# Left-over tokens carried by the last chunk of a batch, and two MoE weights loaded through two hardware queues

## The chip, the cores and the metric

The kernel runs on one core of a Trainium2 chip. The metric is the time of one execution in microseconds of the device; lower is better. The core's 16 DMA engines take work from three kinds of queue that matter here: GpSimd's software queue (q0 in the profile), SyncE's hardware queue (q1) and ScalarE's hardware queue (q10).

## What is computed

The inputs q, k, v are float32 of shape (4, 6208, 256): B = 4 batches, N = 6208 tokens, C = 256 channels. An attention between channels is followed by a mixture-of-depths layer, in which only the 128 tokens of a batch with the highest score pass a small MLP:

```python
qn = q / (norm(q, axis=1) + 1e-06);  kn = k / (norm(k, axis=1) + 1e-06)
a = softmax(kn.transpose(0, 2, 1) @ qn / tau)        # 256 x 256 for each batch
x = v @ a                                            # (4, 6208, 256)
scores = x @ w_gate;  out = x.copy()
for b in range(B):
    top = indices of the 128 highest scores[b]
    ye = maximum(x[b, top] @ w1, 0) @ w2             # 256 -> 1024 -> 256
    out[b, top] = x[b, top] + sigmoid(scores[b, top])[:, None] * ye
```

## The kernel before

**Tiling.** A batch of 6208 tokens is cut into `NFULL` = 6 chunks of `CHUNK` = 1024 tokens and `REM` = 64 left-over tokens. A chunk is laid over 128 partitions with `RPP` = 8 consecutive tokens each, so that a partition reads 8 KB in one piece from memory; the load casts to bfloat16 and writes 4 KB to a partition. The 64 left-over tokens are a seventh piece (chunk index `NFULL`): one token on each of 64 partitions, in small tiles of their own (`rem_pool`), loaded by a DMA of its own (L179). All loads of q, k and v are issued by GpSimd (`emit_load`, L168 to L187). The chunk (q, k) of the last batch that is used last is loaded in two halves of four tokens a partition (L185).

**Two passes.** Pass 1 reads q and k of a batch and sums three products over all tokens (L303, L305, L307): q against k, and the squared norms. From these come the 256 x 256 weights `a` (`softmax_stages`). Pass 2 transposes v on TensorE (L414), copies it to `vt_sb` (L418, L420), multiplies by `a` (L485) and copies the float32 result into a `stage` tile (L493, L491), which SyncE stores (`emit_store`, L559): 8 KB for each of 128 partitions, 1 MB a chunk. The left-over tokens have a stage tile and a store of their own (64 KB). A score for each token comes from L439; `select_stages` narrows down a threshold in seven rounds on VectorE and turns the 128 hits into row numbers (`idx`); GpSimd gathers those rows of v (L660), `mlp_stages` runs the MLP, and GpSimd scatters the updated rows over the stored output (L729), which has to come after the stores of that batch.

**Order of work.** The order on TensorE is the list `plan`, written out by hand. The order of loads follows from it (`units`); `pump` issues loads ahead within limits: four (q, k) chunks, six v chunks, two left-over pieces of each kind, and in all 11 pieces ahead. Side work (softmax, selection, MLP) is slipped in between by `spent`. With the batches numbered 0 to 3, the names in the code are H = 1, E = 2, L = 3. Chunk 3 of batch 1 and all of batch 2 are not stored when they are ready but put in `deferred`, and `flush_deferred` (L779) stores them behind the last loads of v: the first of them in four pieces, of which the first and third wait for loads named by their place from the end of `units` (L784). The stores of batch 3 follow. The last two chunks of batch 1 (`LATE`) come at the very end: there the MLP's update isn't scattered but added to the stage tile by a matmul against a one-hot matrix (`late_onehot`, `late_mm`, `late_pair`), and the last of them is stored in two halves (`next_late`, L882).

**The start.** `emit_weights` loads w1 (1 MB, L218) and w2 (1 MB, L224) through SyncE's queue into two stage tiles, and ScalarE casts them (L220, L225). The gate vector of 1 KB comes through ScalarE's queue (L211).

Of the kernel before, what the change touches and what calls it, by code (L numbers as in the profile page):

```python
# [17 lines left out]
P = 128  # L18
# [8 lines left out]
def kernel(  # L27
# [30 lines left out]
    ST_BUFS = 8  # L58
    VT_BUFS = 22
    EARLY = 4  # L60
# [27 lines left out]

    def view(t, b, ci):
        if ci < NFULL:  # L90
            return t[b, ci * CHUNK:(ci + 1) * CHUNK, :].rearrange("(p s) c -> p s c", s=RPP)
        return t[b, NFULL * CHUNK:N, :]

# [55 lines left out]
    plan += T[6:8] + W + T[8:10] + S[:6] + T[10:] + rest[2:3] + [("side",)] + S[6:]  # L149
    rest = rest[3:]  # L150
    units = []
    for op in plan:
        if op[0] in ("p1", "T"):
            u = ("qk", op[1], op[2]) if op[0] == "p1" else ("v", op[1], op[2][0])
            if u not in units:
                units.append(u)
    loaded = {}
    load_inst = {}
    state = {"next": 0, "qk": 0, "v": 0, "qkr": 0, "vr": 0}
    ahead = [0]  # L160
    limit = {"qk": QK_BUFS, "v": V_BUFS, "qkr": 2, "vr": 2}

    def bucket(kind, ci):
        return kind if ci < NFULL else kind + "r"

    halved = ("qk", B - 1, NFULL - 1)

    def emit_load(u):  # L168
        kind, b, ci = u
        tiles = []  # L170
        for nm, src in ((("q", q), ("k", k)) if kind == "qk" else (("v", v),)):
            if ci < NFULL:
                pool = qk_pool if kind == "qk" else v_pool
                t = pool.tile([P, RPP, C], BF16, name=f"{nm}_ch")
                if u != halved:
                    ins = nc.gpsimd.dma_start(out=t, in_=view(src, b, ci))  # L176
            else:
                t = rem_pool.tile([P, 1, C], BF16, name=f"{nm}_rem")
                ins = nc.gpsimd.dma_start(out=t[:REM, 0, :], in_=view(src, b, ci))  # L179
            tiles.append(t)  # L180
        if u == halved:
            h = RPP // 2
            for half in (slice(0, h), slice(h, RPP)):
                for t, src in zip(tiles, (q, k)):
                    ins = nc.gpsimd.dma_start(out=t[:, half, :], in_=view(src, b, ci)[:, half, :])  # L185
        loaded[u] = tiles
        load_inst[u] = ins  # L187

    def pump(most=1000):
        while state["next"] < len(units) and most > 0:  # L190
            u = units[state["next"]]
            bk = bucket(u[0], u[2])
            if state[bk] >= limit[bk] or ahead[0] >= AHEAD:
                return
            emit_load(u)
            ahead[0] += 2 if u[0] == "qk" else 1
            state[bk] += 1
            state["next"] += 1
            most -= 1

    def consumed(u):
        state[bucket(u[0], u[2])] -= 1
        ahead[0] -= 2 if u[0] == "qk" else 1
        pump()
# [5 lines left out]
    wg_row = moe.tile([P, D], F32, name="gy")[0:1, :]  # L210
    nc.scalar.dma_start(out=wg_row, in_=moe_w_gate.partition_broadcast(1))  # L211

    def emit_weights():


        assert C * F == P * RPP * C
        raw = st_pool.tile([P, RPP, C], F32, name="stage").rearrange("p a c -> p (a c)")
        nc.sync.dma_start(out=raw.rearrange("p (k n) -> p k n", n=F), in_=moe_w1.rearrange("(k p) n -> p k n", p=P))  # L218
        for kc in range(C // P):
            nc.scalar.copy(w1_sb[:, kc, :, :],  # L220
                           raw[:, kc * F:(kc + 1) * F].rearrange("p (n f) -> p f n", f=NFC))
        raw = st_pool.tile([P, RPP, C], F32, name="stage").rearrange("p a c -> p (a c)")
        raw = raw.rearrange("p (f n) -> p f n", n=D)
        nc.sync.dma_start(out=raw, in_=moe_w2.rearrange("(p f) n -> p f n", f=NFC))  # L224
        nc.scalar.copy(w2_sb, raw)  # L225

    emit_weights()


# [29 lines left out]
    nc.vector.memset(wrow, 1.0)  # L259
    nc.vector.memset(wrow[:, :, RPP - 1:NCOL - 1:RPP], float(CHUNK - RPP + 1))  # L260
    nc.vector.memset(wrow[:, :, NCOL - 1:NCOL], 0.0)
# [5 lines left out]
    for i in range(NSTEP):  # L267
# [11 lines left out]
    nc.vector.tensor_copy(rhs[:, NCOL + 2:NCOL + 3], iota_col)  # L279
    ones_col = const.tile([P, NCOL], BF16)  # L280
# [7 lines left out]
    def p1_steps(b, ci):  # L288
# [3 lines left out]
        s_ps, g_ps = acc[b]  # L292
        qt, kt = loaded[("qk", b, ci)]
        rows = RPP if ci < NFULL else 1
        parts = P if ci < NFULL else REM

        def step(s):
            first = ci == 0 and s == 0
            last = ci == NFULL
            qs, ks = qt[:parts, s, :], kt[:parts, s, :]  # L300
# [106 lines left out]
    def p2_transpose(b, g, on_act=False):  # L407
        ci, s0, n = g
        parts = P if ci < NFULL else REM
        vt = loaded[("v", b, ci)][0]  # L410
        vt_ps = vt_psum()
        for j in range(n):
            for cc in range(2):
                nc.tensor.transpose(vt_ps[:, cc, j, :parts], in_=vt[:parts, s0 + j, cc * P:(cc + 1) * P],  # L414
                                    identity=ident_b[:parts, :parts])
# [116 lines left out]
    def late_onehot(idx):  # L532

        base = float(H * N + LATE[0] * CHUNK)
        at = moe.tile([P, 1], F32, name="late_at")
        nc.vector.tensor_copy(at, idx)
        nc.vector.tensor_scalar(out=at, in0=at, scalar1=-base, scalar2=1.0 / RPP, op0=ALU.add, op1=ALU.mult)
        onehot = moe.tile([P, len(LATE), RPP, P], BF16, name="late_onehot")
        for i in range(len(LATE)):
            at_row = moe.tile([P, RPP], F32, name=f"late_at_row{i}")  # L540
            nc.vector.tensor_scalar(out=at_row, in0=iota_row[:, 0:RPP], scalar1=-1.0 / RPP, scalar2=at,
                                    op0=ALU.mult, op1=ALU.add)
            nc.vector.tensor_tensor(out=onehot[:, i, :, :], in0=iota_row[:, None, :].to_broadcast([P, RPP, P]),
                                    in1=at_row[:, :, None].to_broadcast([P, RPP, P]), op=ALU.is_equal)
            if i + 1 < len(LATE):
                nc.vector.tensor_scalar(out=at, in0=at, scalar1=-float(P), scalar2=None, op0=ALU.add)
        late_moe.append(onehot)

    def emit_store(b, ci, rows=(0, RPP), count=1):
        st = stage_of[(b, ci)]  # L550
        pieces = []
        if ci == NFULL:
            pieces.append((view(out, b, ci), st[:REM, 0, :]))
        else:
            n = (rows[1] - rows[0]) // count
            for r in range(rows[0], rows[1], n):
                pieces.append((view(out, b, ci)[:, r:r + n, :], st[:, r:r + n, :]))
        for dst, src in pieces:
            ins = nc.sync.dma_start(out=dst, in_=src)  # L559
# [10 lines left out]
    def select_stages(b):  # L570
# [55 lines left out]
        with nc.allow_low_precision(reason="counts of at most 49 are whole in bf16"):  # L626
# [25 lines left out]
        fl = moe.tile([P, 1], F32, name="fl")  # L652
        nc.vector.scalar_tensor_tensor(out=fl, in0=toff, scalar=float(b * N + NFULL * CHUNK) - 0.5,
                                       in1=mps[:, NCOL + 1:NCOL + 2], op0=ALU.is_lt, op1=ALU.mult)
        idx = moe.tile([P, 1], I32, name="idx", bufs=3)
        nc.vector.tensor_scalar(out=idx, in0=mps[:, NCOL + 2:NCOL + 3], scalar1=fl, scalar2=toff,
                                op0=ALU.max, op1=ALU.add)
        yield
# [120 lines left out]
    def flush_deferred():  # L779
# [3 lines left out]
        emit_store(*deferred.pop(0), count=4)  # L783
        for piece, u in ((first, units[-4]), (first + 2, units[-3])):  # L784
            tc.add_manual_dep(
# [8 lines left out]
    def do_p1(b, ci, s):  # L794
        if s == 0:
            pump()
            using(("qk", b, ci))
        steps = p1_steps(b, ci)
        steps[s]()
        spent(0.43)  # L800
        if s == len(steps) - 1:
            consumed(("qk", b, ci))

    def do_transpose(b, g, on_act=False):
        using(("v", b, g[0]))
        vts[(b, g)] = p2_transpose(b, g, on_act)
        if g[1] == 4 or g[0] == NFULL:
            consumed(("v", b, g[0]))
        spent(0.11 * g[2])
# [131 lines left out]
```

## Time and profile before

| | |
|---|---|
| time, three runs | 261.95 us (261.92 to 263.41) |
| span of the profiled run | 260.1 us |
| busy: TensorE matmul, VectorE, ScalarE, GpSimd | 78%, 49%, 32%, 21% |
| mean granted TensorE clock | 0.947 |
| read from HBM, written to HBM | 78.91 MB, 25.95 MB |
| loads of q, k, v of whole chunks | 72, of which 2 in halves |
| loads of left-over tokens | 12, of 32 KB written to the core's memory each |
| stores of left-over tokens | 4, of 64 KB each |

A page of the profile has the busy share of each engine in 40 equal slices (a digit is tenths), the DMA queues with their packets and bytes, the chain of work that ended last, and the instructions in groups with their line, their operands, the mean time of one and the idle time ahead of them. A load's size is given by what it writes, so a chunk of q counts as 512 KB although 1 MB is read for it.

### The profile page before, as it was taken

The numbers are of one execution on the slowest core, as the hardware profiler recorded it, in microseconds if no ns is written. First come the engines' busy times: TensorE is split into PE (matmuls) and PEld (weight loads), VectorE is DVE, ScalarE is ACT, GpSimd is POOL, SyncE is SP. The second block draws the span as 40 slices with busy tenths as digits, with TensorE's granted clock in tenths as the row PEclk, the third lists the DMA queues.
The fourth block names the chain that finished last, engine by engine and source line by source line (L and its number), as shares of the span: only waits on it lengthen the run. The fifth ranks groups of instructions, "written<-read, shape, count | busy, mean of one in ns | idle before, by whom it ended". The sixth has DMA issues, their size and how long they took to land.

```text
span 260.1 us, 6113 instructions
## 1 busy us (share of the span) xinstructions
PE 201.7 (78%) x2586; PEld 177.3 (68%) x2586; DVE 126.9 (49%) x474; ACT 84.3 (32%) x149; POOL 55.6 (21%) x104
## 2 busy tenths in 40 slices
PE   0199668889938688698997888799999878889920
PEld 0088557789927476598996677698999668568710
DVE  0300003624403366622436888666685865887830
ACT  3700000167720000107770100434110964878010
POOL 7104124121110023222300325230334003001110
PEclk9999999999976589689999999999999999999995
DMA  7999999999999999999999999999999999999980
GB/s 240 262 213 212 212 212 214 215 214 281 317 317 317 304 213 213 214 212 210 292 316 273 214 212 223 212 213 214 212 210 212 217 257 419 402 412 391 415 369 1
DMA packets 17181, 66.84 MB, mean 257 GB/s; under 512 B 2050, under 2 KB 3587, under 8 KB 14211
## 3 DMA queue, kind: packets, MB, share of 16 engines
q0 software_dynamic: 12384, 38.93, 75.0%
q1 hardware_dynamic: 4768, 27.53, 26.2%
q8 instruction: 20, 0.33, 0.4%
q14 instruction: 7, 0.05, 0.0%
q10 hardware_dynamic: 2, 0.00, 0.0%
HBM read 78.91 MB, written 25.95 MB: 403 GB/s over the span
## 4 chain that ended last, share of the span: by engine, by line
DMA 57%; PE 16%; issue 15%; DVE 6%; POOL 2%; POOLq 1%; ACT 0%
DMA k_ch<-in_k_dram 22%; DMA q_ch<-in_q_dram 18%; DMA v_ch<-in_v_dram 12%; PE s_ps L303 4%; PE o_ps L485 4%; DMA out_dram<-upd,idx 3%; DMA out_dram<-stage 2%; PE g_ps L307 2%; PE g_ps L305 2%; PE vt_ps L414 2%; DVE cnt L610 1%; DVE cmp L606 1%; PE sc_ps L439 1%; DVE junk L322 1%; PE m_ps L354 1%
## 5 line engine op out<-in xcount | busy, mean ns | idle before, releaser
L303 PE MATMUL s_ps<-q_ch,k_ch 128*128 128x256 bf16 x384 | 95.4, 289 | 20.9 <-DMA k_ch<-in_k_dram 20.3
L305 PE MATMUL g_ps<-q_ch 128*128 128x128 bf16 x384 | 88.1, 229 | 1.1 <-DVE nsq L322 1.0
L307 PE MATMUL g_ps<-k_ch 128*128 128x128 bf16 x384 | 88.1, 229 | 0.0
L303 PEld LDWEIGHTS <-k_ch 128*128 128x128 bf16 x384 | 39.7, 103 | 26.8 <-DMA k_ch<-in_k_dram 23.9
L485 PE MATMUL o_ps<-a_sb,vt_sb 128*128 128x256 bf16 (+1 forms) x322 | 47.1, 271 | 2.0 <-ACT vt_sb L418 1.3
L493 ACT COPY stage<-o_ps 128x512 f32<-128x512 f32 x75 | 42.2, 590 | 15.9 <-PE o_ps L485 15.8
L307 PEld LDWEIGHTS <-k_ch 128*128 128x128 bf16 x384 | 39.7, 103 | 8.2 <-issue 1.6
L305 PEld LDWEIGHTS <-q_ch 128*128 128x128 bf16 x384 | 39.6, 103 | 1.2 <-issue 0.9
L420 DVE COPY vt_sb<-vt_ps 128x1024 bf16<-128x1024 bf16 (+1 forms) x35 | 22.2, 637 | 31.5 <-PE vt_ps L414 31.5
L485 PEld LDWEIGHTS <-vt_sb 128*128 128x128 bf16 (+1 forms) x392 | 30.5, 97 | 8.3 <-issue 4.5
L318 ACT COPY s_sb<-s_ps 128x512 f32<-128x512 f32 x4 | 2.3, 585 | 85.3 <-PE s_ps L303 55.1
L439 PEld LDWEIGHTS <-vt_sb 128*128 128x128 bf16 x392 | 25.3, 96 | 2.7 <-DVE sc L574 0.2
L414 PEld LDWEIGHTS <-v_ch 128*128 128x128 bf16 x384 | 22.2, 97 | 5.6 <-DMA v_ch<-in_v_dram 4.4
L439 PE MATMUL sc_ps<-aw_sb,vt_sb 128*128 128x2 bf16 x392 | 25.7, 164 | 0.0
L176 POOL DMA_DIRECT2D q_ch<-in_q_dram x23 | 12.7, 553 | 60.3 <-PE g_ps L307 40.6
L414 PE MATMUL vt_ps<-ident_b,v_ch 128*128 128x128 bf16 x336 | 24.6, 219 | 1.2 <-ACT vt_sb L418 0.7
L322 DVE CUSTOM_DVE_ANT_0 junk<-g_ps,ident_f 128x128 bf16<-128x128 f32 x16 | 4.6, 290 | 34.8 <-PE g_ps L307 34.4
L176 POOL DMA_DIRECT2D v_ch<-in_v_dram x24 | 12.8, 539 | 23.8 <-DMA q_ch<-in_q_dram 11.0
L176 POOL DMA_DIRECT2D k_ch<-in_k_dram x23 | 12.5, 544 | 22.8 <-PE o_ps L485 10.6
L418 ACT COPY vt_sb<-vt_ps 128x1024 bf16<-128x1024 bf16 x11 | 10.6, 1012 | 14.1 <-PE vt_ps L414 14.0
L610 DVE TENSOR_REDUCE cnt<-cmp 128x7 bf16<-128x343 bf16 x28 | 14.4, 513 | 1.0
L606 DVE SCALAR_TENSOR_TENSOR cmp<-u,delta,shares 128x343 bf16<-128x343 f32 x24 | 13.9, 579 | 0.9
(161 smaller groups left out, 214.5 us busy)
## 6 DMA issues: line engine op xcount, KB each, us to landing
out_dram<-stage SPq DMA_DIRECT2D x22, 1024.0 KB, 8.0
v_ch<-in_v_dram POOLq DMA_DIRECT2D x24, 512.0 KB, 14.8
q_ch<-in_q_dram POOLq DMA_DIRECT2D x23, 512.0 KB, 16.8
k_ch<-in_k_dram POOLq DMA_DIRECT2D x23, 512.0 KB, 16.9
stage<-in_moe_w_dram SPq DMA_DIRECT2D x2, 1024.0 KB, 7.0
out_dram<-stage SPq DMA_DIRECT2D x4, 256.0 KB, 5.6
out_dram<-stage SPq DMA_DIRECT2D x2, 512.0 KB, 6.2
q_ch<-in_q_dram POOLq DMA_DIRECT2D x2, 256.0 KB, 9.0
```

What stands on the lines that cost most here:

```text
L176: ins = nc.gpsimd.dma_start(out=t, in_=view(src, b, ci))
L303: nc.tensor.matmul(s_ps[:, cc, :], lhsT=ks[:, sl], rhs=qs, start=first and cc == 0, stop=last and cc == 1)
L305: nc.tensor.matmul(g_ps[:, cc, :], lhsT=qs[:, sl], rhs=qs[:, sl], start=first and cc == 0, stop=False)
L307: nc.tensor.matmul(g_ps[:, 2 + cc, :], lhsT=ks[:, sl], rhs=ks[:, sl], start=False, stop=last and cc == 1)
L414: nc.tensor.transpose(vt_ps[:, cc, j, :parts], in_=vt[:parts, s0 + j, cc * P:(cc + 1) * P], identity=ident_b[:parts, :parts])
L418: nc.scalar.copy(vt_sb[:, :, :n, :parts], vt_ps[:, :, :n, :parts])
L420: nc.vector.tensor_copy(vt_sb[:, :, :n, :parts], vt_ps[:, :, :n, :parts])
L439: nc.tensor.matmul(sc_ps[:parts, col, :], lhsT=vt_sb[:, cc, j, :parts], rhs=aw_sb[:, cc, :], start=cc == 0 and col in (0, NCOL - 1), stop= ...
L485: nc.tensor.matmul(o_ps[:parts, pj, :], lhsT=vt_sb[:, cc, j, :parts], rhs=a_sb[:, cc, :], start=pj == 0 and cc == 0, stop=pj == m - 1 and ...
L493: nc.scalar.copy(st[:parts, s0 + pair * 2:s0 + pair * 2 + m, :], o_ps[:parts, :m, :])
L606: nc.vector.scalar_tensor_tensor(out=cmp, in0=wide, scalar=delta, in1=thr, op0=ALU.subtract, op1=ALU.is_ge)
L610: nc.vector.tensor_reduce(out=cnt, in_=cmp, axis=AX.X, op=ALU.add)
```

## The change

It has two parts. In the first the 64 left-over tokens are no piece of their own in memory any more. The last chunk of a batch now has 1088 tokens: partitions 0 to 63 take nine consecutive tokens each and partitions 64 to 127 eight. Because the two halves have different strides in memory, everything that moves this chunk between memory and the core is split in two DMAs, one of 64 partitions (`lo`) and one of the other 64 (`hi`). The ninth token is still handled as a step of its own by TensorE and still has its own stage tile and store, but its loads, tiles and places in `units` are gone. The tiles of q, k and v get a ninth row; room for it comes from two `vt_sb` buffers. The formulas from partition and place to row number (`wrow`, `rhs`, `fl`, `idx`, `late_onehot`) follow the new layout. The purpose is to be rid of 12 small loads.

In the second part w2 goes through ScalarE's hardware queue while w1 goes through SyncE's, both at once, and the gate vector goes through SyncE's behind w1.

```diff
-    VT_BUFS = 22
+    VT_BUFS = 20
...
+    def pieces(t, b, ci, rows):
+        if ci < NFULL - 1:
+            v = t[b, ci * CHUNK:(ci + 1) * CHUNK, :].rearrange("(p s) c -> p s c", s=RPP)
+            return [(v[:, rows[0]:rows[1], :], slice(0, P), slice(*rows))]
+        mid = (NFULL - 1) * CHUNK + REM * (RPP + 1)
+        lo = t[b, (NFULL - 1) * CHUNK:mid, :].rearrange("(p s) c -> p s c", s=RPP + 1)
+        got = [(lo[:, rows[0]:rows[1], :], slice(0, REM), slice(*rows))]
+        if rows[0] < RPP:
+            hi = t[b, mid:N, :].rearrange("(p s) c -> p s c", s=RPP)
+            rows = (rows[0], min(rows[1], RPP))
+            got.append((hi[:, rows[0]:rows[1], :], slice(REM, P), slice(*rows)))
+        return got
...
     def emit_load(u):
...
+        tiles = [pool.tile([P, RPP + 1, C], BF16, name=f"{nm}_ch") for nm, _ in srcs]
+        top = RPP + (ci == NFULL - 1)
+        for rows in [(0, RPP // 2), (RPP // 2, top)] if u == halved else [(0, top)]:
+            for t, (_, src) in zip(tiles, srcs):
+                for dram, parts, rr in pieces(src, b, ci, rows):
+                    ins = nc.gpsimd.dma_start(out=t[parts, rr, :], in_=dram)
...
-    nc.scalar.dma_start(out=wg_row, in_=moe_w_gate.partition_broadcast(1))
     def emit_weights():
+        raw1 = st_pool.tile([P, RPP, C], F32, name="stage").rearrange("p a c -> p (a c)")
+        nc.sync.dma_start(out=raw1.rearrange("p (k n) -> p k n", n=F), in_=moe_w1.rearrange("(k p) n -> p k n", p=P))
         raw = st_pool.tile([P, RPP, C], F32, name="stage").rearrange("p a c -> p (a c)")
...
+        nc.scalar.dma_start(out=raw, in_=moe_w2.rearrange("(p f) n -> p f n", f=NFC))
...
     emit_weights()
+    nc.sync.dma_start(out=wg_row, in_=moe_w_gate.partition_broadcast(1))
...
     def emit_store(b, ci, rows=(0, RPP), count=1):
...
             for r in range(rows[0], rows[1], n):
-                pieces.append((view(out, b, ci)[:, r:r + n, :], st[:, r:r + n, :]))
+                for dram, parts, rr in pieces(out, b, ci, (r, r + n)):
+                    todo.append((dram, st[parts, rr, :]))
...
-        for piece, u in ((first, units[-4]), (first + 2, units[-3])):
+        for piece, u in ((first, units[-3]), (first + 2, units[-2])):
```

In `late_onehot`, which runs once, on VectorE, two instructions go and five come: the first token of each partition (one of 128 x 128 for the chunk before the last, two for the last) and one more of 128 x 8 for each of the two chunks.

More of the change, by code (lines that the diff above doesn't have):

```diff
@@ L87 @@
     out_flat = out.rearrange("b n c -> (b n) c")
[L89 to L92, printed above, removed]
+    def pieces(t, b, ci, rows):
[10 more added lines that the diff above has]
+        return got
     def groups(ci):
@@ L150, with home @@
     rest = rest[3:]
+    def home(ci):
+        return min(ci, NFULL - 1)
     units = []
@@ L153 @@
         if op[0] in ("p1", "T"):
-            u = ("qk", op[1], op[2]) if op[0] == "p1" else ("v", op[1], op[2][0])
+            u = ("qk", op[1], home(op[2])) if op[0] == "p1" else ("v", op[1], home(op[2][0]))
             if u not in units:
@@ L158 @@
     load_inst = {}
-    state = {"next": 0, "qk": 0, "v": 0, "qkr": 0, "vr": 0}
+    state = {"next": 0, "qk": 0, "v": 0}
     ahead = [0]
-    limit = {"qk": QK_BUFS, "v": V_BUFS, "qkr": 2, "vr": 2}
-    def bucket(kind, ci):
-        return kind if ci < NFULL else kind + "r"
+    limit = {"qk": QK_BUFS, "v": V_BUFS}
     halved = ("qk", B - 1, NFULL - 1)
@@ L169, in emit_load @@
         kind, b, ci = u
[L170 to L185, printed above, removed]
+        srcs = (("q", q), ("k", k)) if kind == "qk" else (("v", v),)
+        pool = qk_pool if kind == "qk" else v_pool
+        tiles = [pool.tile([P, RPP + 1, C], BF16, name=f"{nm}_ch") for nm, _ in srcs]
[4 more added lines that the diff above has]
+                    ins = nc.gpsimd.dma_start(out=t[parts, rr, :], in_=dram)
         loaded[u] = tiles
@@ L191, in pump @@
             u = units[state["next"]]
-            bk = bucket(u[0], u[2])
+            bk = u[0]
             if state[bk] >= limit[bk] or ahead[0] >= AHEAD:
@@ L201, in consumed @@
     def consumed(u):
-        state[bucket(u[0], u[2])] -= 1
+        state[u[0]] -= 1
         ahead[0] -= 2 if u[0] == "qk" else 1
@@ L210 @@
     wg_row = moe.tile([P, D], F32, name="gy")[0:1, :]
-    nc.scalar.dma_start(out=wg_row, in_=moe_w_gate.partition_broadcast(1))
     def emit_weights():
         assert C * F == P * RPP * C
+        raw1 = st_pool.tile([P, RPP, C], F32, name="stage").rearrange("p a c -> p (a c)")
+        nc.sync.dma_start(out=raw1.rearrange("p (k n) -> p k n", n=F), in_=moe_w1.rearrange("(k p) n -> p k n", p=P))
         raw = st_pool.tile([P, RPP, C], F32, name="stage").rearrange("p a c -> p (a c)")
-        nc.sync.dma_start(out=raw.rearrange("p (k n) -> p k n", n=F), in_=moe_w1.rearrange("(k p) n -> p k n", p=P))
+        raw = raw.rearrange("p (f n) -> p f n", n=D)
+        nc.scalar.dma_start(out=raw, in_=moe_w2.rearrange("(p f) n -> p f n", f=NFC))
         for kc in range(C // P):
             nc.scalar.copy(w1_sb[:, kc, :, :],
[L221 to L224, printed above, removed]
+                           raw1[:, kc * F:(kc + 1) * F].rearrange("p (n f) -> p f n", f=NFC))
         nc.scalar.copy(w2_sb, raw)
     emit_weights()
+    nc.sync.dma_start(out=wg_row, in_=moe_w_gate.partition_broadcast(1))
     ident_f = const.tile([P, P], F32)
@@ L259 @@
     nc.vector.memset(wrow, 1.0)
-    nc.vector.memset(wrow[:, :, RPP - 1:NCOL - 1:RPP], float(CHUNK - RPP + 1))
+    nc.vector.memset(wrow[:, :, RPP - 1:NCOL - 2:RPP], float(CHUNK - RPP + 1))
     nc.vector.memset(wrow[:, :, NCOL - 1:NCOL], 0.0)
@@ L278 @@
                             scalar2=None, op0=ALU.mult)
-    nc.vector.tensor_copy(rhs[:, NCOL + 2:NCOL + 3], iota_col)
+    nc.vector.tensor_scalar(out=rhs[:, NCOL + 2:NCOL + 3], in0=iota_col, scalar1=float(REM),
+                            scalar2=None, op0=ALU.min)
     ones_col = const.tile([P, NCOL], BF16)
@@ L292, in p1_steps @@
         s_ps, g_ps = acc[b]
-        qt, kt = loaded[("qk", b, ci)]
+        qt, kt = loaded[("qk", b, home(ci))]
         rows = RPP if ci < NFULL else 1
@@ L299, in step @@
             last = ci == NFULL
-            qs, ks = qt[:parts, s, :], kt[:parts, s, :]
+            row = s if ci < NFULL else RPP
+            qs, ks = qt[:parts, row, :], kt[:parts, row, :]
             for cc in range(2):
@@ L409, in p2_transpose @@
         parts = P if ci < NFULL else REM
-        vt = loaded[("v", b, ci)][0]
+        vt = loaded[("v", b, home(ci))][0]
+        row = s0 if ci < NFULL else RPP
         vt_ps = vt_psum()
@@ L413, in p2_transpose @@
             for cc in range(2):
-                nc.tensor.transpose(vt_ps[:, cc, j, :parts], in_=vt[:parts, s0 + j, cc * P:(cc + 1) * P],
+                nc.tensor.transpose(vt_ps[:, cc, j, :parts], in_=vt[:parts, row + j, cc * P:(cc + 1) * P],
                                     identity=ident_b[:parts, :parts])
@@ L532, in late_onehot @@
     def late_onehot(idx):
-        base = float(H * N + LATE[0] * CHUNK)
         at = moe.tile([P, 1], F32, name="late_at")
         nc.vector.tensor_copy(at, idx)
-        nc.vector.tensor_scalar(out=at, in0=at, scalar1=-base, scalar2=1.0 / RPP, op0=ALU.add, op1=ALU.mult)
+        first = moe.tile([P, D], F32, name="gy")[:, 0:P]
         onehot = moe.tile([P, len(LATE), RPP, P], BF16, name="late_onehot")
-        for i in range(len(LATE)):
+        for i, ci in enumerate(LATE):
+            if ci < NFULL - 1:
+                nc.vector.tensor_scalar(out=first, in0=iota_row, scalar1=float(RPP), scalar2=None, op0=ALU.mult)
+            else:
+                nc.vector.tensor_scalar(out=first, in0=iota_row, scalar1=float(REM), scalar2=None, op0=ALU.min)
+                nc.vector.scalar_tensor_tensor(out=first, in0=iota_row, scalar=float(RPP), in1=first,
+                                               op0=ALU.mult, op1=ALU.add)
             at_row = moe.tile([P, RPP], F32, name=f"late_at_row{i}")
-            nc.vector.tensor_scalar(out=at_row, in0=iota_row[:, 0:RPP], scalar1=-1.0 / RPP, scalar2=at,
-                                    op0=ALU.mult, op1=ALU.add)
-            nc.vector.tensor_tensor(out=onehot[:, i, :, :], in0=iota_row[:, None, :].to_broadcast([P, RPP, P]),
+            nc.vector.tensor_scalar(out=at_row, in0=iota_row[:, 0:RPP], scalar1=float(H * N + ci * CHUNK),
+                                    scalar2=None, op0=ALU.add)
+            nc.vector.tensor_scalar(out=at_row, in0=at_row, scalar1=-1.0, scalar2=at, op0=ALU.mult, op1=ALU.add)
+            nc.vector.tensor_tensor(out=onehot[:, i, :, :], in0=first[:, None, :].to_broadcast([P, RPP, P]),
                                     in1=at_row[:, :, None].to_broadcast([P, RPP, P]), op=ALU.is_equal)
-            if i + 1 < len(LATE):
-                nc.vector.tensor_scalar(out=at, in0=at, scalar1=-float(P), scalar2=None, op0=ALU.add)
         late_moe.append(onehot)
@@ L550, in emit_store @@
         st = stage_of[(b, ci)]
-        pieces = []
+        todo = []
         if ci == NFULL:
-            pieces.append((view(out, b, ci), st[:REM, 0, :]))
+            dram, parts, _ = pieces(out, b, NFULL - 1, (RPP, RPP + 1))[0]
+            todo.append((dram, st[parts, :, :]))
         else:
@@ L556, in emit_store @@
             for r in range(rows[0], rows[1], n):
-                pieces.append((view(out, b, ci)[:, r:r + n, :], st[:, r:r + n, :]))
-        for dst, src in pieces:
+                for dram, parts, rr in pieces(out, b, ci, (r, r + n)):
+                    todo.append((dram, st[parts, rr, :]))
+        for dst, src in todo:
             ins = nc.sync.dma_start(out=dst, in_=src)
@@ L652, in select_stages @@
         fl = moe.tile([P, 1], F32, name="fl")
-        nc.vector.scalar_tensor_tensor(out=fl, in0=toff, scalar=float(b * N + NFULL * CHUNK) - 0.5,
-                                       in1=mps[:, NCOL + 1:NCOL + 2], op0=ALU.is_lt, op1=ALU.mult)
+        nc.vector.scalar_tensor_tensor(out=fl, in0=toff, scalar=float(b * N + (NFULL - 1) * CHUNK) - 0.5,
+                                       in1=mps[:, NCOL + 2:NCOL + 3], op0=ALU.is_ge, op1=ALU.mult)
         idx = moe.tile([P, 1], I32, name="idx", bufs=3)
-        nc.vector.tensor_scalar(out=idx, in0=mps[:, NCOL + 2:NCOL + 3], scalar1=fl, scalar2=toff,
-                                op0=ALU.max, op1=ALU.add)
+        nc.vector.tensor_scalar(out=idx, in0=mps[:, NCOL + 1:NCOL + 2], scalar1=fl, scalar2=toff,
+                                op0=ALU.add, op1=ALU.add)
         yield
@@ L796, in do_p1 @@
             pump()
-            using(("qk", b, ci))
+            using(("qk", b, home(ci)))
         steps = p1_steps(b, ci)
@@ L800, in do_p1 @@
         spent(0.43)
-        if s == len(steps) - 1:
-            consumed(("qk", b, ci))
+        if s == len(steps) - 1 and ci != NFULL - 1:
+            consumed(("qk", b, home(ci)))
     def do_transpose(b, g, on_act=False):
-        using(("v", b, g[0]))
+        using(("v", b, home(g[0])))
         vts[(b, g)] = p2_transpose(b, g, on_act)
-        if g[1] == 4 or g[0] == NFULL:
-            consumed(("v", b, g[0]))
+        if (g[1] == 4 and g[0] != NFULL - 1) or g[0] == NFULL:
+            consumed(("v", b, home(g[0])))
         spent(0.11 * g[2])
```

## The prediction

> **What bounds the kernel now.** I read the busy slices first, then the queues, the stages, the waits at the end. The busy slices (DMA share, and GB/s by the bytes that are written):
>
> ```profile
> DMA  7999999999999999999999999999999999999980
> GB/s 240 262 213 212 212 212 214 215 214 281 317 317 317 304 213 213 214 212 210 292 316 273 214 212 223 212 213 214 212 210 212 217 257 419 402 412 391 415 369 1
> ```
>
> The DMA engines are busy from the second slice to the last but one; no compute engine is. The rate has two levels that are one: a load writes half of what it reads, so 213 GB/s of loads is 426 GB/s of reading, and pure stores run at 391 to 419. The queues and some stretches (the columns of a stretch: its length, busy time of PE, PEld, DVE, ACT, POOL with counts, granted clock, DMA share, GB/s):
>
> ```profile
> q0 software_dynamic: 12384, 38.93, 75.0%
> q1 hardware_dynamic: 4768, 27.53, 26.2%
> ```
>
> ```profile
> 13.00:60.00 47.00, 38.96 (x491) 34.97 (x492) 8.28 (x35) 6.92 (x14) 11.70 (x22) 1.00 1.06 213
> 216.00:230.00 14.00, 12.03 (x148) 9.75 (x146) 10.89 (x42) 10.05 (x20) 2.02 (x2) 1.00 1.03 413
> 240.00:250.00 10.00, 8.40 (x85) 6.65 (x81) 8.07 (x19) 2.49 (x6) 0.98 (x1) 1.00 1.01 416
> ```
>
> Loads own the engines up to 215 us; then 15 MB of stores that were held back (chunk 3 of batch 1, all of batch 2, all of batch 3, the two late chunks of batch 1) run with nothing beside them until 254. So time in DMA is time of the kernel, at both ends. What follows the last byte is fixed:
>
> ```profile
> SPq L936 <- DMA out_dram<-upd,idx: 5.1, 1, 5.1
> SPq L936 <- PEq L936: 5.0, 2, 4.5
> ```
>
> The last scatter starts at 250.6 and lands near 255.5; the last stores end at 254; a closing step of 4.5 us leads to 260.1. The scatter is a second chain of the same length, but it waits for the stores of batch 3, so a store queue that grows pushes both.
>
> The issues of DMAs that the change touches (count, KB each, us to landing):
>
> ```profile
> out_dram<-stage SPq DMA_DIRECT2D x22, 1024.0 KB, 8.0
> ...
> out_dram<-stage SPq DMA_DIRECT2D x2, 512.0 KB, 6.2
> ...
> q_rem<-in_q_dram POOLq DMA_DIRECT2D x4, 32.0 KB, 19.9
> k_rem<-in_k_dram POOLq DMA_DIRECT2D x4, 32.0 KB, 17.1
> v_rem<-in_v_dram POOLq DMA_DIRECT2D x4, 32.0 KB, 16.8
> ```
>
> [...] This trace has no large transfer of 64 partitions, but the 64 KB stores of left-over tokens are such[...]. Near 230.6 us most 1 KB packets took 46 ns, yet two engines that ran in step took 72 to 82 ns for each of four (starts 230.576, .650, .727, .802 and 230.584, .656, .730, .804): 2 x 1024 B in 75 ns is 27.3 GB/s. [...] SyncE's two issues at 0.81 and 1.32 us cost 0.45 us each, and w2's packets follow w1's without a gap.
>
> **The change, part by part.**
>
> *Loads saved.* 12 loads of 64 packets of 512 B go: 768 packets. Packet records, fitted over stretches of 3 us with loads alone, give an engine 308 ns for a packet of 4096 B, 158 for 2048, 46 for 512 (check: 128 x 308 / 16 = 2.46 us a chunk, and 524,288 B at 213 GB/s is 2.46). That is 8.5 ns a packet plus 0.0732 ns a byte. The bytes stay, as a ninth row of packets that exist anyway; only the 8.5 ns go: 768 x 8.5 / 16 = **0.4 us**. If a 4608 B packet is cut in two, 0; if the ninth row came free, 768 x 46 / 16 = 2.2. I take 0.4. The number of load DMAs is the same (two for each tensor and batch, eight instead of six for the halved pair), so GpSimd's 0.53 us an issue is not more but for two, under a queue that is 15 us deep.
>
> *Loads of 64 partitions.* [...] I take 0; the upper end is 5% of 12 x 2.5 us, 1.5 us.
>
> *Stores in halves.* The store of the last chunk of each batch becomes two of 64 partitions, in one queue, with 8 KB packets as before. [...] A half of 0.52 MB at 8 x 27.3 = 218 GB/s takes 2.4 us, and 1.27 at 414: 1.15 us more a half, **2.3 a chunk** if the engines run in step; 0 if the two of each pair are apart by more than a half. How far apart they run is seen at the left-over stores: their packets start over 0.85 us in the first, and in the second ten engines start within 0.4 us and six 1.2 us later. Most pairs overlap for most of a half, and the slowest pair sets the end. So I take 2.0 for chunk 5 of batch 2 and 2.0 for that of batch 3, both in the pure stores after 215. The late chunk 5 of batch 1 goes out in two times two pieces with 4 KB packets, 0.6 us each, which a drift of half a us takes apart more easily: 1.2 of 2.3. Batch 0's goes out at 72 to 101 us between loads; an engine then stores half of the time[...]: 0.3. Sum 5.5, ends 1 and 8. Nothing hides it: queued behind it in SyncE's queue are all later stores, and behind those of batch 3 GpSimd's last scatter.
>
> *Weights.* The engines are full with w1 and w2 from 1.9 us on, the first q packet comes at 5.7, and 2 MB are 2 MB in one queue or two. w1 took 3.27 us for 1 MB (320 GB/s) because first packets took up to 1 us; a second queue beside it may fill some of that: 0 to 0.7, I take 0.2. The gate vector behind w1 lands later, perhaps at 9 us; TensorE's small product (6.87 now) and a chain of VectorE constants to 10.1 wait for it, but the first chunk arrives only at 13.15. Cost 0. ScalarE's casts are needed from 210 on.
>
> *The rest.* `vt_sb` 22 to 20: the 12th and 13th transposes of batch 3 reuse buffers of products that come earlier in the list. Three more VectorE instructions in `late_onehot`, some 0.6 us where VectorE is half idle. Places in `units`: the same loads of v are meant. One entry less each for TensorE's waits. All 0, hidden by the DMA queue.
>
> Sum: 5.5 - 0.4 - 0.2 = +4.9; 261.95 + 4.9 = **266.8 us**.
>
> **The rivals.** *Ports don't bind (A):* [...] only the savings stay: 261.95 - 0.6 = 261.3. For it: most 1 KB packets on 64 partitions were not slowed. Against: those that met were, and a phase of 1.27 us is seven times as long as four such packets. *Ports bind in full (B):* 3 x 2.3 + 1 + 1 for the loads - 0.6 = +8.3, 270.2. [...] Against: the measured drift. *The ninth row is free (C):* 2.2 + 0.7 saved and ports as in A, 259.0; and the last v piece lands earlier by as much. Against: packet time is linear in bytes, and reading runs at 26.6 GB/s an engine already. A and C end on the other side. *A wait takes over (D):* GpSimd's scatter of batch 2, ahead of that of batch 3, or SyncE's eight more issues of 0.33 us in a queue that waits on its own; the first moves with the stores, the second is behind a backlog of 5 us. It adds 1 at most to the forecast.
>
> **How the numbers follow.** Forecast with its sizes between 263.5 and 269: 0.64. A: 0.22. B: 0.08. C: 0.06. The range leaves out C, most of B and A's best end: 260.9 to 269.3. Faster by over 1% (under 259.3) is C: 0.06. Within 1% (to 264.6) is A and the low end of the forecast, with two of its stores off step: 0.22 + 0.06 = 0.28. Slower: 0.66.
>
> **What would show it.** In the profile after: q1 has packets of 8 KB near 600 ns at the last chunks of batches 2 and 3; the GB/s of one or two slices between 222 and 258 us fall from above 400 towards 300; the loads end 0.5 us earlier, near 214.7; the stretch from there to the last store grows from 39 us to some 44. If the pure stores keep 410 GB/s, the port step is wrong; if the loads' 213 GB/s falls in chunk 5, the step on the loads is; if the loads end over 2 us earlier, the price of the small packets is.

## The result and the profile after

The changed kernel takes 265.4 us (265.23 to 266.23), the kernel before in the same session 261.94. The ratio is 1.0127, with a 95% interval of 1.0084 to 1.017: it is slower by 3.3 us, between 2.2 and 4.5. The forecast was 266.8 us and slower. Runs of one kernel fall into two groups some 1.5 us apart (the kernel before near 262.0 and near 263.5), so a median can jump from one to the other, and the differences below are worked out from the ratios on record.

The busy slices of the kernel after, DMA share and GB/s:

```profile
DMA  6999999999999999999999999999999999989990
GB/s 237 259 211 216 211 214 210 218 211 283 310 323 314 301 217 213 214 213 213 334 324 217 212 214 213 222 212 214 214 195 215 214 355 401 382 348 397 305 326 9
```

The engines are as busy as before, but in the pure stores the rate now falls to 348, 305 and 326 in single slices, where the lowest was 369 before. The queues after:

```profile
q0 software_dynamic: 11648, 38.93, 73.5%
q1 hardware_dynamic: 4706, 26.48, 26.1%
q10 hardware_dynamic: 144, 1.05, 1.1%
```

The software queue has 736 packets fewer for the same 38.93 MB (the 768 of 512 B are gone, and two more DMAs bring 16 closing packets of 4 B each), and w2 is in q10. The stretches that the prediction showed of before, and then two around the last chunks of batch 2 and batch 3 (columns as there: length, busy PE, PEld, DVE, ACT, POOL, clock, DMA share, GB/s):

```profile
13.00:60.00 47.00, 38.84 (x486) 34.57 (x486) 9.60 (x62) 11.57 (x16) 11.70 (x22) 1.00 1.06 213
216.00:230.00 14.00, 12.03 (x153) 9.81 (x151) 10.60 (x41) 9.55 (x19) 2.01 (x2) 1.00 1.03 404
240.00:250.00 10.00, 8.94 (x94) 7.19 (x91) 7.89 (x22) 2.95 (x7) 0.99 (x1) 1.00 1.01 347
```

```profile
228.00:234.00 6.00, 4.84 (x46) 3.90 (x45) 4.88 (x20) 4.54 (x9) 0.00 (x0) 1.00 0.89 305
246.00:252.00 6.00, 3.59 (x40) 2.66 (x37) 3.55 (x11) 1.29 (x3) 0.00 (x0) 1.00 1.01 274
```

The same two stretches of the kernel before:

```profile
228.00:234.00 6.00, 4.84 (x47) 3.88 (x45) 4.83 (x21) 4.89 (x10) 0.00 (x0) 1.00 1.00 406
246.00:252.00 6.00, 3.05 (x35) 2.21 (x32) 3.01 (x10) 1.29 (x3) 0.97 (x1) 1.00 1.01 420
```

The loads keep their 213; the stores fall from 406 and 420 GB/s to 305 and 274, with the DMA engines reported about as busy. Busy is not moving: the packet records show what happens in them. Before, 4 of the 1323 store packets of 8 KB after 222 us took over 450 ns, the rest 309 to 350 nearly all. After, 134 of 1339 did, with a heap at 634 ns (median of those between 560 and 660 from 246 to 252 us). One packet of 8192 B in 309 ns is 26.5 GB/s, and two in 634 ns are 25.8: that is what two engines show that share the rate of one. The records don't name the engine of a packet, so the pairs are inferred from these times.

Where the time came in is read from the clock at which all queues but GpSimd's had begun a given number of MB. From 18 to 20 MB (chunk 5 of batch 2 lies there) it went from 4.93 us to 6.46; from 24 to 26 MB (chunk 5 of batch 3) from 5.06 to 7.05; from 27 MB to the last store packet from 3.47 to 4.45. Together that is 4.5 us, more than the 3.3 of the times; the profiled run of the changed kernel was its longest (266.23, against 262.14 for the profiled run of before). The last store packet ends at 259.02 instead of 253.74. The loads end at 214.97 instead of 215.29, where the last one of before is a left-over piece; its last whole chunk had landed at 214.67. The DMA issues of stores, and the waits at the end:

```profile
out_dram<-stage SPq DMA_DIRECT2D x19, 1024.0 KB, 9.8
...
out_dram<-stage SPq DMA_DIRECT2D x6, 512.0 KB, 7.3
out_dram<-stage SPq DMA_DIRECT2D x8, 256.0 KB, 7.2
v_ch<-in_v_dram POOLq DMA_DIRECT2D x4, 288.0 KB, 18.3
```

```profile
SPq L950 <- DMA out_dram<-upd,idx: 4.8, 1, 4.8
SPq L950 <- PEq L950: 4.0, 2, 3.5
```

A whole store of 1 MB now needs 9.8 us from issue to landing instead of 8.0; with whole stores again in the changed kernel (below) it is 7.2. The last scatter starts at 254.2 instead of 250.6, here before and after:

```profile
250.64 0.97 POOL L729 DMA_INDIRECT out_dram<-upd,idx  x1 [6.61 <-DVE upd L723]
254.18 0.97 POOL L743 DMA_INDIRECT out_dram<-upd,idx  x1 [9.61 <-issue]
```

Before, it followed the MLP's update and the landing of the scatter ahead of it (249.87 and 249.85). After, the update is ready at 250.4, and the scatter waits 3.8 us longer, for the stores of batch 3. The closing step was 1 us shorter in this profile (3.5 for 4.5), so the span grew by 4.3 us, not 5.3.

### The profile page after: what moved, and what is told of

It is laid out like the page before. It is cut to its first block, busy times and chain, and to the rows that moved or that the text cites. A ratio compares the mean times of both kernels' runs of the same rounds, so it can differ in the third digit from the quotient of the medians.

```text
span 264.4 us, 6134 instructions
## 1 busy us (share of the span) xinstructions
PE 200.8 (76%) x2586; PEld 177.6 (67%) x2586; DVE 127.5 (48%) x477; ACT 84.2 (32%) x149; POOL 56.6 (21%) x106
## 3 DMA queue, kind: packets, MB, share of 16 engines
q0 software_dynamic: 11648, 38.93, 73.5%
## 4 chain that ended last, share of the span: by engine, by line
PE 42%; DMA 21%; DVE 17%; issue 10%; ACT 4%; POOLq 1%; SPq 0%; POOL 0%; DVEq 0%
DMA k_ch<-in_k_dram 17%; PE s_ps L309 10%; PE o_ps L492 9%; PE vt_ps L421 6%; PE g_ps L313 5%; PE g_ps L311 5%; DMA q_ch<-in_q_dram 3%; DVE cnt L624 3%; ACT vt_sb L425 3%; DVE cmp L620 3%; PE sc_ps L446 2%; DVE junk L328 1%; PE m_ps L631 1%; PE m_ps L360 1%; ACT stage L500 1%
## 5 line engine op out<-in xcount | busy, mean ns | idle before, releaser
L309 PE MATMUL s_ps<-q_ch,k_ch 128*128 128x256 bf16 x392 | 97.2, 288 | 17.8 <-DMA k_ch<-in_k_dram 13.8
L311 PE MATMUL g_ps<-q_ch 128*128 128x128 bf16 x392 | 89.8, 229 | 1.9 <-DVE nsq L328 1.9
L313 PE MATMUL g_ps<-k_ch 128*128 128x128 bf16 x392 | 89.7, 229 | 0.0
L309 PEld LDWEIGHTS <-k_ch 128*128 128x128 bf16 x392 | 40.4, 103 | 23.6 <-DMA k_ch<-in_k_dram 17.6
L313 PEld LDWEIGHTS <-k_ch 128*128 128x128 bf16 x392 | 40.5, 103 | 9.1 <-issue 2.5
L311 PEld LDWEIGHTS <-q_ch 128*128 128x128 bf16 x392 | 40.3, 103 | 1.7 <-issue 1.4
L188 POOL DMA_DIRECT2D q_ch<-in_q_dram x30 | 16.5, 552 | 69.7 <-PE g_ps L313 49.0
L421 PE MATMUL vt_ps<-ident_b,v_ch 128*128 128x128 bf16 (+1 forms) x344 | 25.5, 218 | 1.3 <-ACT vt_sb L425 0.7
L188 POOL DMA_DIRECT2D k_ch<-in_k_dram x30 | 16.2, 543 | 45.4 <-DMA k_ch<-in_k_dram 15.9
L421 PEld LDWEIGHTS <-v_ch 128*128 128x128 bf16 x392 | 23.1, 97 | 2.0 <-issue 1.4
L188 POOL DMA_DIRECT2D v_ch<-in_v_dram x28 | 14.9, 533 | 25.0 <-DMA q_ch<-in_q_dram 12.1
```

The lines of the kernel that those rows point to most:

```text
L188: ins = nc.gpsimd.dma_start(out=t[parts, rr, :], in_=dram)
L309: nc.tensor.matmul(s_ps[:, cc, :], lhsT=ks[:, sl], rhs=qs, start=first and cc == 0, stop=last and cc == 1)
```

## The experiments

The theory, that of the ports in the prediction and the expectations: while a store of 64 partitions runs, pairs of engines share the rate of one, and this is the whole loss. It is an inference from the packet times above (634 ns where 309 are usual); what makes two engines share was not shown. What can be tested is where the loss stands and with which cut it comes and goes. The rivals: the loads of 64 partitions, the rows of nine tokens in memory, the number of DMAs, the weights. All experiments but three start from the kernel before. Differences of 0.2% should not be read: the control below, which should do nothing, came out at 0.9979.

**Whole stores in the changed kernel.** The store of the last chunk goes back to one DMA of 128 partitions.

```diff
-                for dram, parts, rr in pieces(out, b, ci, (r, r + n)):
-                    todo.append((dram, st[parts, rr, :]))
+                whole = out[b, ci * CHUNK:(ci + 1) * CHUNK, :].rearrange("(p s) c -> p s c", s=RPP)
+                todo.append((whole[:, r:r + n, :], st[:, r:r + n, :]))
```

> The changed kernel with its loads and weights as they are, but the last chunk of a batch is stored in one DMA of 128 partitions with 8 rows each, as before the change, and the left-over rows in their old place. The rows of the last chunk so reach other places of the output than the reference has. Port theory [...]: all of the loss lies in these stores, so 261.2 us (261.95 less 0.4 for the loads and 0.2 for the weights), and no 8 KB packet near 600 ns after 222 us. Rival, the loss lies in the loads of 64 partitions or in the two weight queues: stays at 265.4.

Measured: 262.75 us, ratio 1.0024 (1.0004 to 1.0045), 0.6 us over before. Most of the loss is gone (it was 3.3), and so are the slow packets: 7 of 1326. The stretch around the last chunk of batch 3:

```profile
246.00:252.00 6.00, 4.41 (x46) 3.16 (x43) 4.59 (x13) 1.29 (x3) 0.00 (x0) 1.00 1.00 416
```

It is back at 416 GB/s (274 in the changed kernel, 420 before). That of batch 2, 228 to 234 us, is at 371 (305 in the changed kernel, 406 before): in this profile TensorE ran at 0.57 of its clock from 216 to 224 us, just ahead of it, so its tail is not compared further. The 0.6 us that the loads and weights were to save are not there; what remains is of the same size the other way, at the edge of what can be read.

**Halves alone, and two controls.** The kernel before, with only the store of the last chunk cut: by partitions in halves, by rows, by partitions in quarters (32 in place of 64).

```diff
-                pieces.append((view(out, b, ci)[:, r:r + n, :], st[:, r:r + n, :]))
+                w = 64 if ci == NFULL - 1 else P
+                for p in range(0, P, w):
+                    pieces.append((view(out, b, ci)[p:p + w, r:r + n, :], st[p:p + w, r:r + n, :]))
```

```diff
-                pieces.append((view(out, b, ci)[:, r:r + n, :], st[:, r:r + n, :]))
+                m = n // 2 if ci == NFULL - 1 else n
+                for r2 in range(r, r + n, m):
+                    pieces.append((view(out, b, ci)[:, r2:r2 + m, :], st[:, r2:r2 + m, :]))
```

> The kernel before, with only this changed: the last chunk of every batch is stored in two DMAs of 64 partitions (0 to 63, 64 to 127). Layout in memory, loads and weights stay. Port theory: the same loss as in the changed kernel without its savings, 265.4 + 0.6 = 266.0 us, slow packets at the last chunks of batches 2, 3 and 1. Rival, the loss comes from the stride of nine rows in memory or from anything in the loads: 262.0.

> The control: the kernel before, the same stores cut in two DMAs by rows (4 and 4 of each partition), all 128 partitions in each. Port theory: [...] no loss, 262.0 us. Rival, it is the number of DMAs in the store queue: as the cut by partitions, 265 to 266.

> The kernel before, the same stores cut in four DMAs of 32 partitions. Port theory: [...] the loss is that of the halves at most, 265 to 266 us, or somewhat less since a phase of 0.6 us is sooner pulled apart by drift. Rival, each narrow DMA costs a fixed piece: twice the loss of the halves, 270.

Measured: halves 265.96 us, ratio 1.0107 (1.0051 to 1.0163); rows 262.07, 0.9979 (0.9962 to 0.9997); quarters 265.46, 1.0115 (1.0058 to 1.0171). The stretches before and at chunk 5 of batch 2, of halves, rows and quarters in turn:

```profile
222.00:228.00 6.00, 5.07 (x45) 3.89 (x43) 5.19 (x18) 5.50 (x12) 0.56 (x1) 1.00 1.03 397
228.00:234.00 6.00, 4.51 (x41) 3.44 (x39) 5.31 (x21) 4.59 (x10) 0.00 (x0) 1.00 0.95 325
```

```profile
222.00:228.00 6.00, 4.74 (x42) 3.43 (x40) 5.19 (x19) 5.08 (x12) 0.00 (x0) 1.00 1.03 404
228.00:234.00 6.00, 4.84 (x46) 3.90 (x44) 4.83 (x20) 4.89 (x10) 0.00 (x0) 1.00 1.01 406
```

```profile
222.00:228.00 6.00, 4.74 (x41) 3.43 (x40) 5.19 (x19) 5.06 (x12) 0.00 (x0) 1.00 1.02 403
228.00:234.00 6.00, 4.84 (x46) 3.89 (x45) 4.83 (x20) 4.89 (x10) 0.00 (x0) 1.00 0.90 307
```

All three have some 400 GB/s ahead of that chunk. In it the rows keep 406, halves and quarters fall to 325 and 307. The rows have as many DMAs as the halves, so it isn't their number; the layout in memory is that of before in all three, so it isn't the stride of nine rows. Nor is it that the rows go out in packets of 4 KB: the late chunk does too, and cut by partitions 52 of its 256 packets took over 230 ns (next experiment), where of the rows' 512 only 8 did. Twice as many, half as wide DMAs cost the same within the intervals, which a fixed price for a narrow DMA can't give. That engines share a rate at 32 partitions as they do at 64 would give it; that was the author's assumption. One rival stays open: a half also writes a stretch of 0.5 MB of memory at a time, where the whole store and each half by rows are spread over 1 MB. That quarters, with 0.25 MB at a time, cost no more speaks against it. No run stored 64 partitions that are spread over the whole 1 MB, which would have told more.

**One chunk at a time.** The cut in halves for chunk 5 of one batch only: the condition becomes `ci == NFULL - 1 and b == E`, and so on.

> The kernel before with chunk 5 of batch 0 alone stored in two DMAs of 64 partitions; that store runs at 90 to 101 us beside loads. Port theory: an engine then spends half its time on stores[...]: no loss, 262.35. Rival, a store in halves costs 1 to 2 us wherever it stands: 263.5 to 264.5.

> The kernel before with chunk 5 of batch 2 alone stored in two DMAs of 64 partitions. In the changed kernel 18 to 20 MB of hardware-queue traffic took 6.46 us, 4.93 before, so 1.5 us more: 263.7 beside 262.2. Rival, the last scatter and not the store queue sets the end, and hides it: 262.2.

> The kernel before with chunk 5 of batch 3 alone stored in two DMAs of 64 partitions. In the changed kernel 24 to 26 MB took 7.05 us, 5.06 before: 2.0 us more, 264.2 beside 262.2. Rival, six such stores cost 6.0 together, so one costs 1.0: 263.2.

> The kernel before with the late chunk 5 of batch 1 alone stored in two DMAs of 64 partitions for each of its two halves by rows. In the changed kernel the time from 27 MB to the last store was 4.45 us, 3.47 before: 1.0 us more, 263.2 beside 262.2. Rival, the last scatter lands later than these stores and hides it: 262.2.

Measured, with the kernel before at 262.2 us: batch 0 262.25 us, 1.0002 (0.9979 to 1.0025); batch 2 264.06, 1.0064 (1.0045 to 1.0082), that is 1.7 us; batch 3 263.01, 1.0022 (0.9993 to 1.005), 0.6 us; the late chunk of batch 1 262.82, 0.9995 (0.9969 to 1.002), nothing that can be told. The stretch of the cut chunk, for batch 2 and then for batch 3 (406 and 420 GB/s before):

```profile
228.00:234.00 6.00, 4.84 (x46) 3.89 (x45) 4.83 (x22) 4.89 (x10) 0.00 (x0) 1.00 0.91 317
246.00:252.00 6.00, 4.35 (x45) 3.11 (x42) 4.52 (x13) 1.29 (x3) 0.00 (x0) 1.00 0.99 287
```

In batch 0 the store stands beside loads (its packets run from 85 to 92 us, earlier than the expectation says), and its stretch moves the same bytes, first before, then with the halves:

```profile
72.00:100.00 28.00, 18.56 (x176) 15.77 (x175) 11.25 (x40) 1.28 (x3) 4.37 (x9) 0.76 1.05 281
```

```profile
72.00:100.00 28.00, 17.08 (x177) 14.65 (x176) 11.26 (x40) 1.36 (x3) 4.38 (x9) 0.88 1.05 281
```

So for this one store beside loads no loss can be told, and between 84 and 95 us one packet of 8 KB took over 450 ns, as in the kernel before; the cost stands where there are only stores. The late chunk goes out in packets of 4 KB, and some of these were slow: 52 of its 256 took over 230 ns, where before none did (usual: 159). What that costs is too small to be told. Nor is the 1.0 us that the changed kernel's profile lost from 27 MB on shown to be the halves' work: two kernels that store the late chunk whole, the one with batch 0 in halves and that of the next experiment, have 4.3 us there too. The sum of the four is 2.2 us, the cut of all of them together cost 2.8 (1.3 to 4.3). Batch 3 is not settled: in the profile of that kernel, its longest run, 24 to 26 MB took 6.56 us, 1.5 more than before, but by the ratio it cost 0.6 (-0.2 to 1.3).

**A larger dose.** All six full chunks of batch 3 in halves.

> A larger dose: the kernel before, with all six full chunks of batch 3 stored in two DMAs of 64 partitions, all other stores whole. Port theory: each costs what chunk 5 of batch 3 cost in the changed kernel (26 MB less 24 MB of stores issued took 7.05 us, 5.06 before), so 6 x 2.0 = 12 us more, 274; at the most 6 x 2.3 = 13.8. Rival, a fixed cost of the last store only: 264 to 265.

Measured: 268.18 us, ratio 1.0191 (1.0135 to 1.0248), 5.0 us for six stores and not 12. The stretch of these stores, before and in this kernel:

```profile
230.00:250.00 20.00, 17.70 (x176) 14.54 (x173) 15.32 (x49) 10.69 (x22) 1.94 (x2) 1.00 1.00 406
```

```profile
230.00:254.00 24.00, 17.69 (x176) 14.54 (x173) 15.32 (x49) 10.70 (x22) 1.95 (x2) 0.95 0.98 298
```

24 us at 298 GB/s are 7.15 MB, which at 406 take 17.6: a loss of 6.4 us, 1.1 a store. (This is the profile of the longest of four runs; by the ratio a store cost 0.8.) A loss that comes with every such store fits the theory, its linear use does not: by the prediction's estimate a pair in step all the time would pay 2.3 a store, so one that meets by chance half of the time 1.15. That the pairs drift apart in a long row of halves fits this number; it was not tested by itself.

**The weights alone.** The kernel before with w2 through ScalarE's queue and the gate vector behind w1, as in the diff of the change.

> The kernel before with the second part of the change alone: w1 by SyncE's queue, w2 by ScalarE's at the same time, the gate vector behind w1. Prediction: 0.2 us less at most, 261.8 to 262.4 beside a kernel before of 262.35. Rival, the shared start delays the first loads for good: 263.

Measured: 262.07 us, ratio 0.9986 (0.9965 to 1.0007): no difference. By the packet records w2 lands at 6.8 us and w1 at 11.2, where before w1 came first and both had landed at 9.7; the first q packet comes at 5.5 instead of 5.7. The gate vector is late: it lands near 11.4 us, behind w1, and TensorE's small product starts at 12.18 in the changed kernel, not at 6.87. First before, then after:

```profile
6.87 1.22 PE L254 MATMUL m_ps<-gy,ones_f 1*128 1x256 f32 x2 [6.87 <-DVE ones_f L235]
13.16 0.40 PE L303 MATMUL s_ps<-q_ch,k_ch 128*128 128x256 bf16 x1 [5.08 <-DMA k_ch<-in_k_dram]
```

```profile
12.18 1.19 PE L257 MATMUL m_ps<-gy,ones_f 1*128 1x256 f32 x2 [12.18 <-DMA gy<-in_moe_w_gate_dram]
13.54 0.40 PE L309 MATMUL s_ps<-q_ch,k_ch 128*128 128x256 bf16 x1 [0.18 <-DMA k_ch<-in_k_dram]
```

The first product of pass 1 follows at 13.54 instead of 13.16. No loss of time comes of it that could be told.

**The loads alone.** The changed kernel with whole stores (as above) and the weights of before; then the same with the last (q, k) chunk of batch 3 not loaded in two halves by rows.

```diff
-        for rows in [(0, RPP // 2), (RPP // 2, top)] if u == halved else [(0, top)]:
+        for rows in [(0, top)]:
```

> The loads of the changed kernel alone: weights as before, the last chunk stored in one DMA of 128 partitions as before (its rows so reach other places of the output than the reference has). The step on the loads said 0.4 us less than before, 261.9 beside 262.35. Rival, loads of 64 partitions [...] eat it up: 262.35 to 263.5.

> The loads of the changed kernel (weights and stores as before, rows of the last chunk so reach other places of the output), with the last q, k chunk of batch 3 no longer loaded in two halves by rows: four DMAs in place of eight. If the eight small DMAs left the load queue too shallow, the 190 GB/s seen at 194 to 198 us come back to 213, and the 0.4 us with them: 262.3, less what the halves were worth for TensorE. Rival, any load of 64 partitions loses on the ports: the dip stays, 262.7.

Measured: loads alone 262.7 us, ratio 1.002 (1.0002 to 1.0038); without the halves by rows 262.36, ratio 0.9981 (0.9964 to 0.9998). Both are as near to 1 as the control by rows (0.9979), so neither is told from the kernel before by its time: the second has a ratio under 1 and yet a median over the 262.2 of before. What can be said is that the 0.4 us of savings were not seen with the loads alone, nor in the kernel with whole stores (1.0024). The traces say more. The stretch in which that chunk is loaded, of before, of the loads alone, and without halves:

```profile
194.00:198.00 4.00, 4.00 (x60) 3.79 (x58) 2.95 (x12) 0.00 (x0) 1.81 (x4) 1.00 1.15 214
```

```profile
194.00:198.00 4.00, 4.00 (x59) 3.80 (x57) 3.56 (x14) 0.81 (x2) 3.25 (x7) 1.00 1.09 190
```

```profile
194.00:198.00 4.00, 4.00 (x59) 3.79 (x57) 3.83 (x14) 0.81 (x2) 1.54 (x4) 1.00 1.05 211
```

Up to 34 MB of loads the new layout was 0.13 us ahead of before (191.32 for 191.45). Then the eight pieces of 128 and 160 KB came, the rate fell to 190, a few packets took up to 1.7 us, and at 36 MB it was 0.23 behind (201.25 for 201.02). With four pieces in place of eight the dip is gone and 36 MB are reached at 200.76, though the last chunk lands no earlier for it (214.74, before 214.67). So in the traces the savings of the loads were lost around the chunk that is cut twice.

The packets tell where. Those of the eight pieces kept their usual 172 to 211 ns, all but two. The late packets are the first ones of v behind them: in the run of the loads alone ten of 4096 B took over 450 ns, usual 324, which is 0.31 us over 16 engines; the changed kernel has eight, also 0.31 us, and before none. GpSimd had issued this v late, because it first waited twice for a landing to issue the last two pieces. Its issues before, then in the changed kernel:

```profile
191.50 0.55 POOL L176 DMA_DIRECT2D v_ch<-in_v_dram  x1 [1.73 <-DMA q_ch<-in_q_dram]
```

```profile
193.82 0.51 POOL L188 DMA_DIRECT2D k_ch<-in_k_dram  x1 [1.93 <-DMA k_ch<-in_k_dram]
194.43 2.44 POOL L188 DMA_DIRECT2D v_ch<-in_v_dram  x4
```

The first packets of this v start near 196 us in both, so 4.5 us after the issue before and some 1.5 us after it now. This speaks for a load queue that ran short, and against pairs of engines that meet in the small pieces; no run changed the one without the other.

## Why the prediction was right

The direction and the cause were right, and the time of 265.4 lies 1.4 us under the forecast. Its sum was +5.5 - 0.4 - 0.2; the whole change measured +3.3 (2.2 to 4.5). That the total (4.9 for 3.3) came nearer than its main term (5.5 for 2.8) is luck: savings that were counted and did not come made up for a part of it.

*Stores in halves.* The step rested on a few 1 KB packets, of two engines at once, that took 75 ns instead of 46, and on the author's assumption that a store from half of the partitions makes eight such pairs of the 16 engines. The runs bear out the loss and where it stands: packets near 634 ns, rates of 274 and 305 GB/s in the stretches named, no loss by rows, none to be told beside loads, the same loss for quarters. The size was 5.5 and measured 2.8 (1.3 to 4.3) alone. The mis-sized terms: batch 2 was put at 2.0 and measured 1.7 (1.2 to 2.2); batch 3 at 2.0, measured 0.6 (-0.2 to 1.3); the late chunk at 1.2, measured -0.1 (-0.8 to 0.5); batch 0 at 0.3, measured nothing. The rule "the slowest pair sets the end" gave too much: of the six stores in a row each cost 1.1 us in the trace and 0.8 by the times, half or less of the 2.3 of engines in step. That the engines drift apart more than was priced is the likely reason; it was not tested.

*Loads saved.* The step failed. It said -0.4, and the loads alone measured +0.5 (0.05 to 1.0), which is too near to the control to be called a loss but is no saving. Its price of a packet fits as far as the last chunk: nine of the twelve small loads are gone by 34 MB, 0.3 us by that price, and all four profiles with the new loads are there before all ten with the old ones (191.23 to 191.38 us, 191.43 to 191.71). What was missed is that the halved pair, eight DMAs instead of six, was dismissed as "not more but for two, under a queue that is 15 us deep". Just there the queue is not deep: GpSimd issues this chunk after a wait of 11.33 us (L185), its small pieces land in 8 to 10 us, and the packets of the v behind them start some 1.5 us after the issue.

*Loads of 64 partitions* were put at 0. In the long run of loads that held (213 GB/s in both). At 211 us, beside the first stores held back, 4608 B packets of the changed kernel took up to 687 ns instead of 361, 0.17 us in all; before, no packet of 4096 B took over its usual 324 there.

*Weights* were put at -0.2; measured -0.4 (-0.9 to 0.2), which says nothing against 0. The gate vector was estimated at 9 us and the small product came at 12.18; the conclusion that it costs nothing at the end stood.

*The second chain* came to bind as said: the last scatter moved with the stores of batch 3. In the kernel before it did not yet wait for them, as the prediction has it, but for the MLP's update and the scatter ahead of it, with a little room. Rival A (no loss in the halves) is excluded by the halves alone (265.96 us), rival B (the full 2.3 us for each store) by the six stores (5.0 us together), rival C (the ninth row free) by the loads alone (262.7 us).

*Two slips without effect.* ScalarE's casts are not needed from 210 us on but from 144.1, where the first MLP multiplies by w1 in the trace of before; they are done at 17.7 after the change. And SyncE has five more issues, 37 for 32, not eight.

## What to carry to other kernels

A DMA that stores from half of the partitions is not half a DMA: where nothing but stores ran, many packets took twice as long (in the changed kernel 134 of 1339 took over 450 ns, with a heap at 634; usual 309) and the rate fell by a fifth to a third (317 for 406 and 274 for 420 GB/s), while the busy share stayed near its height (0.91 for 1.00 and 1.01 for 1.01). If a tile has to be cut, cut it by rows within a partition, which was free here (262.07 us, ratio 0.9979), or put the narrow piece where loads run beside it, where one such store cost nothing that could be told (ratio 1.0002). A saving by merging small loads is worth the packets' fixed part alone (an estimate from the load packets here: 8.5 ns each, 0.4 us for 768), so ask first what the merged shape does to the stores, and whether more and smaller DMAs leave the queue behind them short.

## What the runs showed that was not expected

The loss of halves is not linear in their number: 1.7 us for one amid whole stores (0.6 for another), 5.0 us for six in a row. And single packets took more than two engines that share the rate of one explain: in the changed kernel 37 store packets of 8 KB took over 660 ns, up to 1428, against a usual 309. At 634 ns for two, three or four packets that share would take 0.95 to 1.3 us (an estimate); no run shows such a group, so that stays a guess.
